# Gate and up products in two fp16 terms instead of two fp32r terms

## The chip, the cores and the metric

The kernel runs on one core of a Trainium2 chip. The metric is the device time of one execution in microseconds (us), lower is better, as the median of several runs.

## The reference

A block of memory-augmented attention and a gated feed-forward layer read the same x and are mixed by a gate. All inputs are fp32.

```python
x: [1, 2048, 576]; 32 heads of 18; 4 segments of 512 rows; F = 4608
g = sigmoid((x * gate_w).sum(-1))
# a: in each segment softmax(q k^T) v, mixed by sigmoid(beta) with what a running
#    memory M = sum phi(k)^T v gives for phi(q); then @ wo
# b:
b = (silu(x @ w_gate) * (x @ w_up)) @ w_down
out = g * a + (1 - g) * b
```

The change is in b: the gate and up products x @ w_gate and x @ w_up, [2048, 576] x [576, 4608] each.

## The kernel before

**Two terms.** TensorE multiplies fp32r, a rounded form of fp32 that takes 4 bytes. To keep the precision of fp32, an operand is split: `split` (L114) copies it to a high term in fp32r on ScalarE (L115) and subtracts that from the source on VectorE for a low term (L116). A product is then three matmuls: high x high, high x low, low x high. The 64 rows of the contraction over 576 that are left after four tiles of 128 are packed: high, low and a repetition stand in one tile of 96 or 128 rows, so that one matmul does them.

**Stage one, segments 0 to 3** (0 to 222 us of the profile, `for s in range(NSEG)`, L564). In each segment nine chains of 14 products (`qk`, products at L138) make q and k, with the update of the memory (`upd_gen`) between chains, and eight value steps (`v_step`, L342) make v, from segment 1 on with reads of the memory (`mem_step`). Work of other engines that is to lie beside a chain is put into the list `mid`, which `qk` calls. In segments 0 to 2 the remainder rows of x for the feed-forward layer are split (`rest_load`, `rest_sum`, `rest_split`, L509 to L526; those of the second half are stored in `xrd`), and the remainder rows of the first 8 tiles of weights (`b_step`). In segment 3, x of the first half is loaded, summed and split (`first_load`, `first_sum`, `first_split`).

**Stage two, the loop over f** (222 to about 1700 us, L1043). Rows of x are taken in two halves of 1024, F in 36 tiles of 128. The gate and up products of one half and one f are made by a Strassen scheme with seven products: `seven` (L1030) does one of them with six matmuls of 128x512 (L1035) and one for the remainder rows (L1038), all fp32r. Sums and differences of weight blocks are made by GpSimd, split (`w_make`, L239: ScalarE L251, VectorE L254) and stored in `wc` for the second half, which fetches them (`w_fetch`). Remainder weights go the same way through `rc` (`r_block`, `r_fetch`). The seven results are combined by copies and sums in three PSUM banks (L1093 to L1119); the gate goes through Silu, is multiplied with up, and the product is split again (`hh`, `hl`). The down products (`down_part`, L874) follow for three f at a time.

Between two `seven` stands one `tick`, which calls `beat`: it first issues what `defer(k, ...)` has put off to this beat, then down products, then a step of attention (`att_gen`; scores at L706 and L753 in bf16, values at L782 and L784 in fp16 and bf16). All engines run their instructions in the order written; there is no scheduler that moves them.

x for the second half is loaded, summed and split around the change of halves (`x_second`), into the same tiles `xo..` (`x_slot(SLOT[j], z)`) that held the first half's operands; ten beats of down products and attention (`BREAK`) cover that.

**The end** (about 1700 to 1782 us). Attention's result is multiplied with wo, mixed with the feed-forward result (`f_load` fetches the first half's) and stored.

Of the kernel before, what the change touches and what calls it, by code (L numbers as in the profile page):

```python
# [15 lines left out]
F16 = mybir.dt.float16  # L16
AF = mybir.ActivationFunctionType
# [3 lines left out]
P = 128  # L21
# [31 lines left out]
SLOT = (0, 3, 2, 1, 4, 6, 5)  # L53
RPOS = (0, 1, 4, 2, 5, 6, 3)
BLOCKS = {3: (4, 5), 6: (6, 7), 9: (8, 9), 12: (10, 11), 15: (12,), 18: (13,), 21: (14,), 24: (15,), 27: (16,), 30: (17,)}
KR = 6 * DH

# [6 lines left out]
def gated_mix(ctx, tc, xT, xrest, wf, wfr, wfh, wd, wv, wo, beta, cmask, ident, bmask, out):  # L64
# [30 lines left out]
    consts.tile([P, 16], F32, name="gap")  # L95
    xo = pool(ctx, "xo", 1)
# [17 lines left out]
    def split(hi, lo, src):  # L114
        nc.scalar.activation(hi, src, AF.Copy)  # L115
        nc.vector.tensor_sub(lo, src, f32(hi))  # L116

# [27 lines left out]
    def xr_tile(j, dtype=F32R):  # L145
        return xo.tile([P, L], dtype, name=f"xr{j}")
# [68 lines left out]
    def op_tile():  # L215
        return wop.tile([P, 2, 2, P], F32R, name="wo_")

    def r_block(h, o):
        i, c = divmod(h, 2)
        a, t = (rp.tile([P, 7, 64], d, name=z, bufs=1) for d, z in ((F32, "rr"), (F32R, "rt")))  # L220
# [7 lines left out]
        def keep(k):  # L228
            d = rc[i, 32 * k:32 * k + 32].rearrange("r f (j n) -> (r f) j n", n=P)
            nc.sync.dma_start(d[:, :, 64 * c:64 * c + 64], f32(t))  # L230

        return [(o, lambda: nc.sync.dma_start(a[:, 0:4], wfh[h - 4])), (o + 2, sums),
                (o + 3, lambda: nc.scalar.activation(t, a, AF.Copy)), (o + 3, lambda: keep(0)), (o + 3, lambda: keep(1)),
                (o + 4, lambda: nc.vector.tensor_sub(t, a, f32(t))), (o + 5, lambda: keep(2))]

    def r_fetch(f):
        nc.sync.dma_start(f32(rhs[f % 2][:96]).rearrange("p j n -> p (j n)"), rc[f // 4, :, f % 4])

    def w_make(f):  # L239
# [9 lines left out]
        def high(j):  # L249
            ops[j] = op_tile()  # L250
            nc.scalar.activation(ops[j][:, 0], src[j], AF.Copy)  # L251

        def low(j):
            nc.vector.tensor_sub(ops[j][:, 1], src[j], f32(ops[j][:, 0]))  # L254

        def keep(j):
            nc.sync.dma_start(wc[f, j], f32(ops[j]).rearrange("p a k n -> p (a k n)"))
# [12 lines left out]
    with ExitStack() as st:  # L270
# [178 lines left out]
        nc.vector.memset(vf[:, :, :, DH:E], 1.0)  # L449
        for i in range(2):  # L450
# [38 lines left out]
        def first_load(n):  # L489
            for q, (b, kt) in enumerate((((0, 0), (1, 0)), ((1, 2), (0, 1)), ((1, 1), (1, 3)), ((0, 2), (0, 3)))[n]):  # L490
                if n < 3:
                    r = qps[1].tile([P, NT * P], F32, name=f"{('qhi', 'qlo')[q]}{n}0")[:, :L]
# [10 lines left out]
        def first_split(j, z):  # L503
            XO[j][z] = x_slot(SLOT[j], z)
            split(XO[j][z][:, 0], XO[j][z][:, 1], rx[{1: (0, z), 4: (1, z), 2: (1, 2 + z), 6: (0, 2 + z)}[j]])
# [3 lines left out]
        def rest_load(h):  # L509
            for b in range(2):  # L510
                t = staging()[:, :2 * L].rearrange("p (a n) -> p a n", n=L)
                nc.sync.dma_start(t, xrest[HALF[h][b]])
                rr[b, 0], rr[b, 1] = t[:, 0], t[:, 1]
# [6 lines left out]
        def rest_split(h, j):  # L520
            raw = rr[((0, 0), (0, 0), (1, 1), (0, 1), (1, 0), (1, 1), (0, 1))[j]]
            XR[j] = xr_tile(j)
            nc.scalar.activation(XR[j], raw, AF.Copy)
            nc.vector.tensor_sub(XR[j][32:64], raw[32:64], f32(XR[j][32:64]))
            if h:
                late.append((xrd[j], f32(XR[j])))  # L526
# [5 lines left out]
        def b_load(i):  # L532
            rb[i] = xr_tile(6 * (i % 2), F32).rearrange("p (j n) -> p j n", n=P)
            nc.sync.dma_start(rb[i], wfr[i])

        def b_sums(i):
            a, b = rb[i], xr_tile(1, F32).rearrange("p (j n) -> p j n", n=P)
# [6 lines left out]
        def b_split(i, z):  # L544
            n = 4 - z
            src = (rb, rs)[z].pop(i)[:, :n].rearrange("p j n -> p (j n)")
            hi, lo = (xr_tile(k + z)[:, :P * n] for k in (2, 4))
# [693 lines left out]
```

## Time and profile before

| | |
|---|---|
| median of 3 runs | 1784.82 us (1784.69 to 1784.87) |
| span of the profiled execution | 1782.1 us, some 2.7 us under the median of the runs |
| TensorE (PE) busy | 1770.7 us, 99% of the span |
| VectorE (DVE), ScalarE (ACT), GpSimd (POOL) busy | 1281.8, 939.6, 831.9 us |
| matmuls / instructions in all | 12381 / 36452 |
| moved by DMA | 352 MB |

The page gives each engine's busy time, slices of the span, the chain of work that ended last (followed back from the last instruction), and groups of instructions by line of the kernel with count, busy time, mean duration and idle time before them. Matmuls are pipelined: one lasts longer than the distance to the next, so that what a product costs is read from start to start. PEld is the loading of weights into TensorE, which overlaps with products. L1035 is line 1035 of the kernel.

### The profile page before, as it was taken

To read this page: it belongs to the slowest core of one execution; us is meant where nothing else is said; L and a number is where in the kernel's file an instruction comes from. 1 tells how busy PE (TensorE), PEld (TensorE's weight loads), DVE (VectorE), ACT (ScalarE), POOL (GpSimd) and SP (SyncE) were. 2 spreads that over 40 slices of the span, in tenths; PEclk is the share of its full clock that TensorE was granted. 3 is DMA by queue.
4 is the path that set the end of the run, shared out by engine and by line. 5 is a ranking of instruction groups with operands and counts; after the bars stand their busy time and mean duration, and the time that the engine had idled before them with its cause. 6 is when DMAs were issued, how large, how long until landed. Compare 5 with 4: busy or idle time off the path is not lost.

```text
span 1782.1 us, 36452 instructions
## 1 busy us (share of the span) xinstructions
PE 1770.7 (99%) x12381; PEld 1521.5 (85%) x12381; DVE 1281.8 (72%) x3309; ACT 939.6 (53%) x1718; POOL 831.9 (47%) x1064
## 2 busy tenths in 40 slices
PE   9999999999999999999999999999999999999999
PEld 7899978888888888888887887887887887888899
DVE  6657666878877777777777777777777778775455
ACT  7766565455645564556456445445445445445411
POOL 4434731444554455445535555555555555454121
PEclk9999999999999999999999999999999999999999
DMA  8645497677657865776496447547546456545644
GB/s 298 212 176 184 153 344 225 189 249 264 217 176 238 265 201 174 243 249 215 137 339 207 153 136 215 150 130 215 155 138 210 141 151 195 160 126 188 204 141 140
DMA packets 249418, 352.02 MB, mean 198 GB/s; under 512 B 90320, under 2 KB 130640, under 8 KB 249232
## 3 DMA queue, kind: packets, MB, share of 16 engines
q1 hardware_dynamic: 249232, 349.69, 61.0%
q8 instruction: 98, 1.61, 0.4%
q14 instruction: 88, 0.72, 0.1%
HBM read 210.72 MB, written 138.87 MB: 196 GB/s over the span
## 4 chain that ended last, share of the span: by engine, by line
PE 94%; DVE 2%; DMA 2%; ACT 1%; issue 1%; SPq 0%; DVEq 0%; ACTq 0%
PE bank L1035 37%; PE bank L874 25%; PE bank L138 12%; PE bank L1038 6%; PE bank L753 4%; PE bank L706 4%; PE bank L782 2%; PE bank L784 1%; PE bank L423 1%; PE bank L377 1%; DMA rh<-rc 1%; DMA wo__23740<-wc 0%; PE bank L947 0%; PE bank L385 0%; DMA draw<-in_wd_dram 0%
## 5 line engine op out<-in xcount | busy, mean ns | idle before, releaser
L874 PE MATMUL bank<-dw,hh 128*128 128x320 f32 (+1 forms) x2304 | 485.8, 303 | 1.6 <-DVE ya L883 1.0
L845 POOL TENSOR_TENSOR p<-pe,p 128x512 f16<-128x512 f32 x320 | 381.1, 1191 | 176.3 <-DVE p L843 115.6
L874 PEld LDWEIGHTS bank<-dw,hh 128*128 128x128 f32 x2304 | 378.1, 189 | 19.2 <-DVE ya L883 2.4
L757 ACT ACTIVATE pe<-bank 128x512 f32<-128x512 f32 x320 | 190.4, 595 | 363.5 <-PE bank L753 333.4
L874 PE MATMUL bank<-dw,hl 128*128 128x320 f32 (+1 forms) x1152 | 340.4, 295 | 1.0 <-DVE hl L116 1.0
L765 POOL TENSOR_SCALAR_AFFINE_SELECT pe<-pe 128x256 f32<-128x256 f32 (+1 forms) x320 | 140.3, 438 | 274.1 <-ACT pe L757 270.7
L713 DVE CUSTOM_DVE_ANT_0 scr<-bank,cm 128x512 bf16<-128x512 f32 (+3 forms) x512 | 247.5, 483 | 20.3 <-PE bank L706 12.3
L883 DVE TENSOR_TENSOR ya<-bank,ya 128x320 f32<-128x320 f32 x352 | 157.1, 452 | 102.1 <-PE bank L874 100.2
L874 PEld LDWEIGHTS bank<-dw,hl 128*128 128x128 f32 x1152 | 217.6, 189 | 1.5 <-DVE hl L116 1.5
L1038 PE MATMUL bank<-xr,rh 128*128 128x512 f32 x504 | 196.3, 390 | 0.9 <-DMA rh<-rc 0.9
L753 PE MATMUL bank<-qst,kst 111*128 111x512 bf16 (+3 forms) x512 | 151.5, 305 | 0.0
L843 DVE CAST p<-pe 128x512 f16<-128x512 f32 x320 | 150.3, 470 | 0.0
L706 PE MATMUL bank<-kst,qst 108*128 108x512 bf16 (+3 forms) x512 | 126.1, 300 | 0.4 <-DVE mb L713 0.4
L247 POOL TENSOR_TENSOR ws<-raw 128x256 f32<-128x256 f32 x72 | 66.7, 926 | 110.2 <-DMA raw<-in_wf_dram 53.8
L973 DVE TENSOR_TENSOR hl<-row,hh 128x512 fp32r<-128x512 f32 x120 | 102.0, 850 | 22.1 <-ACT hh L972 21.7
L1038 PEld LDWEIGHTS bank<-xr,rh 128*128 128x128 f32 x504 | 94.6, 188 | 21.6 <-issue 1.3
L1103 ACT ACTIVATE row<-bank 128x512 f32<-128x512 f32 x72 | 43.1, 599 | 125.7 <-PE bank L1038 125.7
L1108 DVE TENSOR_TENSOR row<-bank,row 128x512 f32<-128x512 f32 x72 | 49.7, 691 | 79.9 <-ACT bank L1107 79.9
L1118 DVE TENSOR_TENSOR row<-bank,row 128x512 f32<-128x512 f32 x72 | 49.6, 689 | 60.4 <-PE bank L1038 58.7
L1107 ACT ACTIVATE bank<-bank 128x512 f32<-128x512 f32 x72 | 41.9, 582 | 96.6 <-PE bank L1038 96.6
L138 PE MATMUL bank<-xo,qhi 128*128 128x512 f32 x288 | 91.0, 396 | 0.4 <-DVE xo L116 0.4
L753 PEld LDWEIGHTS <-kst 111*128 111x128 bf16 x512 | 48.3, 97 | 43.3 <-issue 24.8
(1688 smaller groups left out, 3997.9 us busy)
## 6 DMA issues: line engine op xcount, KB each, us to landing
rh<-rc SPq DMA_DIRECT2D x72, 336.0 KB
dc<-dw SPq DMA_DIRECT2D x36, 576.0 KB
dw<-dc SPq DMA_DIRECT2D x36, 576.0 KB
raw<-in_wf_dram SPq DMA_DIRECT2D x72, 256.0 KB
stk<-q SPq DMA_DIRECT2D x32, 384.0 KB
draw<-in_wd_dram SPq DMA_DIRECT2D x36, 288.0 KB
rc<-rt SPq DMA_DIRECT2D x42, 224.0 KB
vd<-vps SPq DMA_DIRECT2D x8, 912.0 KB
```

Of the source, the lines that this page charges most:

```text
L138: nc.tensor.matmul(t, st[n], mv[n], start=(n == 0), stop=(n == 13))
L706: nc.tensor.matmul(t[:, c:c + w], qs[:KR, pr, P * i:P * i + P], ks[:KR, pr, 0:w], start=True, stop=True)
L713: nc.vector.tensor_tensor_reduce(scr[:, :w], t[:, c:c + w], cm[:, L - w:L], 1.0, -3.0e38, OP.add, OP.max, m[:, k:k + 1])
L753: nc.tensor.matmul(t[:, c:c + w], ks[:KR + 3, pr, P * j:P * j + P], qs[:KR + 3, pr, P * j:L], start=True, stop=True)
L757: nc.scalar.activation(pe, t, AF.Exp, scale=SCALE)
L765: nc.gpsimd.affine_select(d, d, pattern=pat, compare_op=OP.is_ge, fill=0.0, base=0, channel_multiplier=-1)
L843: nc.vector.tensor_copy(p1, pe)
L845: nc.gpsimd.tensor_sub(p2, pe, p1)
L874: nc.tensor.matmul(t, p, q[:, cs], start=(f == CH * c and n == 0), stop=(f == CH * c + CH - 1 and n == 2))
L883: nc.vector.tensor_add(ya[:, i, cs], t, ya[:, i, cs])
L1035: nc.tensor.matmul(t, w[:, p, z], x[z][:, q], start=first and n == 0, stop=False, skip_group_check=True)
L1038: nc.tensor.matmul(t, rem[:, RPOS[j]], XR[j], start=False, stop=True, skip_group_check=True)
```

## The change

- The operands of `seven`, weights and x, become fp16: a high term fp16(k * a) and a low term fp16(k * a - high). Before splitting they are scaled by a power of two k: `sx` for x, `sw[i]` for each group of four f. Count and shape of the matmuls are the same. The tiles, `wc` and `rc` take half the bytes.
- The powers are found on the chip. `square` sums squares along a row on ScalarE, `total` adds these sums on VectorE, `power` adds over the partitions with a one-column matmul against ones and makes a power of two from the exponent bits. For x this reads the tiles of segments 0 to 2. The weights of the first 8 f are loaded for it in segment 1 (`look`), those of the others in the first half's loop (`glance`: one group of four f ahead of its use, 2 or 3 loads and squares in each f from pos 0 to 20).
- The scale is taken out again: `iw` = 1 / (sw * sx) is the scale of the Silu, and of the split of w_down (`d_split`).
- Splits use `scalar_tensor_tensor` (source times k, minus the high term) in place of a subtraction.
- First half: j = 0, 3 and 5 used tiles of segments 2 and 3 as they stood; they now have splits of their own. The remainder rows of the first half are loaded and split in segment 3, those of the second half in the loop from pos FT - 6 on (`rest_second`); `xrd` is gone. The two steps j = 6 move from after the value steps into them.
- Remainder weights (`b_step`) move from segments 0 and 1 to segment 2.
- With half the bytes, the x operands of both halves fit side by side (`PLACE`, `x_home`), so those of the second half have homes of their own.

```diff
+TOP = 2.0 ** 76
+SX, SW, IW, ONE = 101, 102, 111, 120
+PLACE = ([[(2, z, 1) for z in range(2)], [(3, z, 0) for z in range(2)], ...
-    wc = dram.tile([FT, 7, P, 4 * P], F32, name="wc")
-    rc = dram.tile([FT // 4, 96, 4, 7 * P], F32, name="rc")
-    xrd = dram.tile([7, P, L], F32, name="xrd")
+    wc = dram.tile([FT, 7, P, 4 * P], F16, name="wc")
+    rc = dram.tile([FT // 4, 96, 4, 7 * P], F16, name="rc")
+    def split_16(hi, lo, src, k):
+        nc.scalar.activation(hi, src, AF.Copy, scale=k)
+        nc.vector.scalar_tensor_tensor(lo, src, k, hi, op0=OP.mult, op1=OP.subtract)
+    def square(src, c):
+        n = src.shape[1]
+        nc.scalar.activation(junk[:, :n], src, AF.Square, accum_out=sc[:, c:c + 1])
+    def total(out, a, b):
+        nc.vector.tensor_reduce(out, sc[:, a:b], axis=AX.X, op=OP.add)
+    def power(out, t):
+        nc.tensor.matmul(t, one.to_broadcast([P, P]), out, start=True, stop=True)
+        nc.vector.tensor_scalar_max(out, t, 1e-24)
+        bits = out.bitcast(I32)
+        nc.vector.tensor_scalar(bits, bits, 24, 127, op0=OP.logical_shift_right, op1=OP.bitwise_xor)
+        nc.vector.tensor_single_scalar(bits, bits, 23, OP.logical_shift_left)
+        nc.vector.tensor_scalar_mul(out, out, TOP)
+    def back(i):
+        nc.vector.tensor_mul(iw[i], sw[i], sx)
+        nc.vector.reciprocal(iw[i], iw[i])
+    def x_home(h, j, z):
+        a, b, c = PLACE[h][j][z]
+        if (a, b) not in homes:
+            homes[a, b] = xo.tile([P, 4, L], F16, name=f"xo{a}{b}")
+        return homes[a, b][:, 2 * c:2 * c + 2]
     def op_tile():
-        return wop.tile([P, 2, 2, P], F32R, name="wo_")
+        return wop.tile([P, 2, 2, P], F16, name="wo_")
         def high(j):
             ops[j] = op_tile()
-            nc.scalar.activation(ops[j][:, 0], src[j], AF.Copy)
+            nc.scalar.activation(ops[j][:, 0], src[j], AF.Copy, scale=sw[f // 4])
         def low(j):
-            nc.vector.tensor_sub(ops[j][:, 1], src[j], f32(ops[j][:, 0]))
+            nc.vector.scalar_tensor_tensor(ops[j][:, 1], src[j], sw[f // 4], ops[j][:, 0], op0=OP.mult, op1=OP.subtract)
         def first_split(j, z):
-            XO[j][z] = x_slot(SLOT[j], z)
-            split(XO[j][z][:, 0], XO[j][z][:, 1], rx[...])
+            XO[j][z] = x_home(0, j, z)
+            src = rx[((0, z), (0, z), (1, 2 + z), (0, 2 + z), (1, z), (1, 2 + z), (0, 2 + z))[j]]
+            split_16(XO[j][z][:, 0], XO[j][z][:, 1], src, sx)
-        FSUM = {4: [(1, 0), (4, 0)], 5: [(2, 0), (1, 1)], 7: [(4, 1), (2, 1)]}
-        FSPLIT = {6: [(1, 0), (4, 0)], 7: [(2, 0), (1, 1)], 8: [(4, 1), (2, 1)]}
+        FSUM = {5: [(1, 0), (4, 0)], 6: [(2, 0), (1, 1)], 8: [(4, 1), (2, 1)]}
+        FSPLIT = {4: [(0, 0)], 5: [(5, 0), (0, 1)], 6: [(1, 0), (4, 0)], 7: [(5, 1), (2, 0), (1, 1)], 8: [(3, 0), (3, 1)]}
...
+                if s == 3:
+                    if n == 1:
+                        mid.append(lambda: total(sx, 0, 20))
+                    if n == 2:
+                        mid.append(lambda: power(sx, lone_tile([P, 1])))
+                        rest_load()
+                        for i in range(2):
+                            mid.append(lambda i=i: back(i))
...
-                    for j, b, kt in ((0, 2, z), (3, 2, 2 + z), (5, 3, 2 + z)):
-                        XO[j][z] = xs_of[b][0][kt]
...
         def d_split(f, r):
-            split_by(1, d[:, 0], d[:, 1], r)
+            k = iw[f // 4]
+            defer(1, lambda: nc.scalar.activation(d[:, 0], r, AF.Copy, scale=k))
+            defer(2, lambda: nc.vector.scalar_tensor_tensor(d[:, 1], r, k, f32(d[:, 0]), op0=OP.mult, op1=OP.subtract))
         def f_load(n):
-            ff = x_slot(n // 2, n % 2, F32).rearrange("p a b -> p (a b)")[:, :D]
+            ff = x_slot(2 + n // 2 if n < 6 else 0, n % 2, F32).rearrange("p a b -> p (a b)")[:, :D]
+        def glance(i, k):
+            f, u = 4 * i + k // 2, k % 2
+            box = []
+            def load():
+                box.append(x_slot(6, k % 2, F32).rearrange("p a b -> p (a b)")[:, :NT * P])
+                nc.sync.dma_start(box[0].rearrange("p (k n) -> p k n", n=P), wf[f][:, u])
+            return [(0, load), (4, lambda: square(box[0], 20 + 9 * i + k))]
+            i = 2 + pos // 3
+            if half == 0 and i < FT // 4:
+                for n in range(3 if pos % 3 < 2 else 2):
+                    plan += [(o + 3 * n - n // 2, fn) for o, fn in glance(i, 3 * (pos % 3) + n)]
+            if half == 0 and pos % 3 == 0 and pos and i <= FT // 4:
+                plan += [(0, lambda i=i: total(sw[i - 1], 11 + 9 * i, 19 + 9 * i)),
+                         (1, lambda i=i: power(sw[i - 1], ts_tile([P, 1]))), (2, lambda i=i: back(i - 1))]
+            if pos == FT - 6:
+                plan += [(o, fn) for o, fn in rest_second(XR2)]
-            nc.scalar.activation(sg0, sg0, AF.Silu)
+            nc.scalar.activation(sg0, sg0, AF.Silu, scale=iw[f // 4])
-            nc.scalar.activation(sg1, y, AF.Silu)
+            nc.scalar.activation(sg1, y, AF.Silu, scale=iw[f // 4])
```

More of the change, by code (lines that the diff above doesn't have):

```diff
@@ L95, in gated_mix @@
     consts.tile([P, 16], F32, name="gap")
+    sc = consts.tile([P, 128], F32, name="sc")
+    junk = consts.tile([P, 640], F16, name="junk")
+    one, sx = sc[:, ONE:ONE + 1], sc[:, SX:SX + 1]
+    sw = [sc[:, SW + i:SW + i + 1] for i in range(FT // 4)]
+    iw = [sc[:, IW + i:IW + i + 1] for i in range(FT // 4)]
     xo = pool(ctx, "xo", 1)
@@ L518, in rest_sum, with rest_split @@
             nc.gpsimd.tensor_sub(o, p, q)
[L520 to L526, printed above, removed]
+        def rest_split(j):
+            XR[j] = xr_home(0, j)
+            rest_16(XR[j], rr[((0, 0), (0, 0), (1, 1), (0, 1), (1, 0), (1, 1), (0, 1))[j]])
         XR = [None] * 7
@@ L656, in gated_mix @@
             start.pop(0)[1]()
-        for z in range(2):
-            first_split(6, z)
     with ExitStack() as st:
```

152 lines of the change are left out of this document (106 added, 46 removed).

## The prediction

> **What bounds the kernel now.** I read the page first: its shares, its slices and the chain of work that ended last.
>
> ```profile
> PE 1770.7 (99%) x12381; PEld 1521.5 (85%) x12381; DVE 1281.8 (72%) x3309; ACT 939.6 (53%) x1718; POOL 831.9 (47%) x1064
> PEclk9999999999999999999999999999999999999999
> PE 94%; DVE 2%; DMA 2%; ACT 1%; issue 1%; SPq 0%; DVEq 0%; ACTq 0%
> PE bank L1035 37%; PE bank L874 25%; PE bank L138 12%; PE bank L1038 6%; PE bank L753 4%; PE bank L706 4%; PE bank L782 2%; PE bank L784 1%; PE bank L423 1%; PE bank L377 1%; DMA rh<-rc 1%; DMA wo__23740<-wc 0%; PE bank L947 0%; PE bank L385 0%; DMA draw<-in_wd_dram 0%
> ```
>
> TensorE is idle 11.4 us of 1782.1, at full granted clock, and 94% of the chain is its own. The lines that change (L1035 and L1038, `seven`) hold 43% of the chain. So a nanosecond saved on each of their products is a nanosecond of the end, as long as the other engines keep up; and no gain can come from waits beyond those 11.4 us. The question is what one such product costs, from start to start. For that I read TensorE in order of time.
>
> ```profile
> 901.01 1.54 PE L1035 MATMUL bank<-xo,wo__11855 128*128 128x512 f32 x6
> 902.39 0.39 PE L1038 MATMUL bank<-xr,rh 128*128 128x512 f32 x1
> 902.62 1.52 PE L1035 MATMUL bank<-xo,wo__11871 128*128 128x512 f32 x6
> 903.98 0.39 PE L1038 MATMUL bank<-xr,rh 128*128 128x512 f32 x1
> 904.20 0.30 PE L874 MATMUL bank<-dw,hh 128*128 128x320 f32 x1
> ...
> 1001.06 0.40 PE L874 MATMUL bank<-dw,hh 128*128 128x256 f32 x2
> 1001.30 0.28 PE L874 MATMUL bank<-dw,hl 128*128 128x256 f32 x1
> 1001.42 0.40 PE L874 MATMUL bank<-dw,hh 128*128 128x256 f32 x2
> ...
> 1001.90 0.38 PE L706 MATMUL bank<-kst,qst 108*128 108x512 bf16 x1
> 1002.12 0.27 PE L753 MATMUL bank<-qst,kst 111*128 111x256 bf16 x1
> ```
>
> Fourteen 4-byte products of 512 columns fill 901.01 to 904.20: 228 ns each, back to back. Three 4-byte products of 256 columns fill 1001.06 to 1001.42: 120 ns each. So 256 columns cost 108 ns, 512 cost 216, and a 4-byte product carries 12 ns that do not depend on its columns. A 2-byte product of 512 columns (L706) starts 0.22 us before the next one.
>
> ```profile
> L1038 PE MATMUL bank<-xr,rh 128*128 128x512 f32 x504 | 196.3, 390 | 0.9 <-DMA rh<-rc 0.9
> L753 PE MATMUL bank<-qst,kst 111*128 111x512 bf16 x128 | 50.0, 390 | 0.0
> L706 PE MATMUL bank<-kst,qst 108*128 108x512 bf16 x128 | 48.7, 381 | 0.4 <-DVE mb L713 0.4
> L1038 PEld LDWEIGHTS bank<-xr,rh 128*128 128x128 f32 x504 | 94.6, 188 | 21.6 <-issue 1.3
> L753 PEld LDWEIGHTS <-kst 111*128 111x128 bf16 x512 | 48.3, 97 | 43.3 <-issue 24.8
> ```
>
> These rows group products and weight loads by shape. At 512 columns the 4-byte product lasts 390 ns, the 2-byte one of L706 381 ns. The L753 one lasts 390, no less than the 4-byte one; at 512 columns it opens its attention step and so follows a 4-byte product, while L706 follows another 2-byte one. A 2-byte weight load lasts 97 ns against 188.
>
> **The change part by part.**
>
> *The products.* 2 halves x 36 x 7 x 7 = 3528 products of 512 columns become 2-byte; their number and columns stay. Saving per product: nothing if they behave like L753's (390 against 390), 12 ns if the whole fixed part goes, 9 ns by L706 (390 - 381, and 228 - 219). I take 9, since six of the seven products of a `seven` follow another 2-byte product, as L706's do: 3528 x 9 = 31.8 us, between 0 and 42.3.
>
> The Trainium skill ("TensorE: Matmul & The Clock Gate", Back-to-back issue gap) gives N / 2.4 + 2.5 ns from start to start, 215.8 ns at 512 columns, with no type in it. The trace's 4-byte 228 ns disagrees with that; if the formula holds for 2-byte products alone, the saving by it is an estimate of 12 ns and 43 us.
>
> *Where types meet.* In the order written out, the stream changes between 4-byte and 2-byte operands 533 times instead of 667, since attention's 2-byte products now stand next to the gate and up products. I price an entry at the 9 ns that L753 shows above L706; 67 pairs of changes fewer are 0.6 us saved.
>
> *Scales on the chip.* Ten one-column products (`power`) stand in TensorE's order. The nearest rows are its four 128-column transposes in 0.44 us (L385), 0.11 us each: 1.1 us. Each waits for VectorE's sum, issued one chain or one tick before it, so I add nothing for the wait; queued behind it are the next products, and if VectorE came 0.5 us late each time it would be 5 us.
>
> ```profile
> 118.52 0.44 PE bank L385 x4
> ```
>
> *Stage one's last segment.* The remainder splits of the first half move into it, and j = 0, 3, 5, which used to borrow the fp32r tiles of x, need splits of their own. The windows are its last chains and its value steps, then two stretches of the loop over f and two disturbed places.
>
> ```profile
> 181.00:202.00 21.00, 21.00 (x115) 18.27 (x114) 9.47 (x19) 10.51 (x19) 14.92 (x16) 1.00 0.37 119
> 202.00:222.00 20.00, 20.00 (x150) 19.66 (x150) 16.31 (x47) 11.37 (x32) 16.77 (x20) 1.00 0.53 186
> 222.00:501.00 279.00, 275.78 (x1672) 236.45 (x1671) 210.71 (x500) 159.76 (x318) 112.16 (x161) 1.00 0.75 251
> 501.00:898.00 397.00, 397.00 (x2695) 344.50 (x2694) 302.66 (x767) 223.14 (x433) 193.47 (x251) 1.00 0.64 211
> 898.00:928.00 30.00, 29.41 (x185) 26.48 (x183) 22.90 (x39) 12.44 (x22) 11.71 (x8) 1.00 1.02 350
> 1660.00:1700.00 40.00, 37.95 (x207) 32.54 (x207) 22.23 (x37) 15.89 (x29) 7.72 (x8) 1.00 0.75 239
> ...
> L116 DVE TENSOR_TENSOR xo<-xo,xo 128x512 fp32r<-128x512 f32 x16 | 12.2, 770 | 2.8 <-ACT xo L115 2.8
> L116 DVE TENSOR_TENSOR xo<-qhi,xo 128x512 fp32r<-128x512 f32 x2 | 2.5, 1238 | 0.0
> L115 ACT ACTIVATE xo<-xo 128x512 fp32r<-128x512 f32 x16 | 9.8, 615 | 0.4 <-DMA xo<-in_xT_dram 0.3
> L518 POOL TENSOR_TENSOR xo<-xo,xo 128x512 f32<-128x512 f32 x6 | 8.5, 1420 | 7.8 <-DVE xr L524 7.8
> ```
>
> The columns after the length are TensorE, weight loads, VectorE, ScalarE, GpSimd. In the chains 11 splits (7 + 6 - 2 that go later) are added, in the value steps 4. ScalarE: 10.51 + 11 x 0.615 = 17.3 of 21 us, room. GpSimd: 14.92 + 4 x 1.42 = 20.6 of 21, just full. VectorE at 0.77 us a split: 9.47 + 8.5 + 16.31 + 3.1 = 37.4 of 41, room; at the 1.24 us that splits of x took in this very stretch (the row with qhi): 9.47 + 13.6 + 16.31 + 5.0 = 44.4 of 41, 3.4 us too much. TensorE waits for VectorE there through its banks, so the bounds are 0 and 5 us; I take 3, by the second row.
>
> The Trainium skill ("GPSIMD Engine Reference", Specifications) says GpSimd's SBUF ports contend with VectorE instructions of two SBUF inputs; 1.24 against 0.77 us agrees, and the new splits still have two such inputs, so by it too the larger figure is the one for this stretch.
>
> *Squares in the loop.* 56 squares of 640 columns (`glance`) are added in the first 21 f; the nearest row is a 640-column copy of 0.73 us: 41 us of ScalarE over some 395 us (21 of 36 f in the 676 us from 222 to 898).
>
> ```profile
> L115 ACT ACTIVATE qhi<-xo 128x640 fp32r<-128x640 f32 x9 | 6.6, 731 | 2.2 <-DMA xo<-in_wf_dram 2.2
>   ACT bank L1093: 2.2, 4
> ...
> L329 DVE TENSOR_TENSOR qr<-bank,q 128x512 f32<-128x512 f32 x36 | 24.8, 688 | 52.3 <-ACT ph L327 38.2 <-ACT q L322 11.6 <-POOL q L333 2.3
> L335 DVE SCALAR_TENSOR_TENSOR ph<-bank,ph 128x512 f32<-128x512 f32 x28 | 19.2, 687 | 0.2
> ```
>
> ScalarE runs there at 57% (159.76 of 279) and goes to 68%. What covers a square is the next `seven` (1.6 us) with what stands between: `a` is copied out at L1093 and is written again only after the next `seven`. Products waited for that copy 4 times, 2.2 us in all. I add 2 us for squares in front of it, 0 to 6. The second half's seven remainder splits, moved from stage one to f = 30 on, find ScalarE at 56% (223.14 of 397): nothing.
>
> Another 38 squares lie in segments 0 to 2.
>
> ```profile
> 88.00:145.00 57.00, 57.00 (x352) 51.87 (x351) 35.69 (x89) 38.02 (x78) 23.62 (x26) 1.00 0.46 160
> ```
>
> At 0.615 us they are 23 us, the 14 remainder copies that leave are 8.6; 15 us more over three segments of some 57 us take ScalarE's 67% to 75%, and three banks of a chain lie between it and TensorE: nothing, 0 to 1 us.
>
> *Splits by scale.* `scalar_tensor_tensor` takes the place of a subtraction: 687 against 688 ns. VectorE, 75% busy at most in the loop, gains nothing and loses nothing.
>
> *Transfers.* Stored operands are halved (wc, rc) and xrd goes; 23 MB of weights are read once more for the squares (72 loads of 256 or 320 KB). With x's second operands in their own homes, their splits no longer wait for the first half's last products. The two disturbed windows hold 0.6 and 2.05 us of idle; I take 1.5 us off, between 0 and 2.7.
>
> *Sum.* - 31.8 - 0.6 + 1.1 + 3 + 2 - 1.5 = - 27.8 us. The profiled span is 1782.1 us, the median 1784.82 (2.7 more, the same before and after): 1757 us.
>
> **The rivals.**
>
> *The whole fixed part goes.* A product at 216 ns: - 42.3 in place of - 31.8, 1746.5 us. For it speaks that the weight load, 188 ns to 97, is all that differs beside the stream; against it that L706 shows 9.
>
> *Type makes no difference to a stream.* All products stay at 228 ns, as L753's 390 would have it: + 1.1 + 3 + 2 - 1.5 = 4.6 us slower, 1789.4. Against it: every 512-column L753 stands behind a 4-byte product. The skill's formula, read for all types alike, would give this as well; the 228 ns speak against that reading.
>
> *Helpers run out.* TensorE waits in stage one and at the copies of L1093 for 10 to 20 us more: 1767 to 1777. For it: GpSimd's 20.6 of 21.
>
> *ScalarE in front of the copies, the other side.* If each of the 56 squares stands fully ahead of a copy that TensorE waits for, they cost 41 us in place of 2: 1757 + 39 = 1796. It turns the sign when more than 40 of the 56 do ((27.8 + 2) / 0.73). Against it: 68% load, and `seven` lasts longer than two ScalarE operations.
>
> **How the numbers follow.** Forecast 50%, whole fixed part 24%, helpers 14%, no difference by type 6%, squares 6%. A difference of 0.2% (3.6 us) is about what a measurement of this kernel can tell from none. The forecast's own range is 1747 to 1766; the first three cases are faster, but 3 points of the helpers' go to an outcome near zero, as does 1 of the last two cases; so faster 0.85, same 0.04, slower 0.11. The range that keeps eight in ten reaches from 1743 (the whole fixed part and all waits at their best, 1784.8 - 42.3 - 0.6 + 1.1 - 2.7 = 1740, cut by its small chance) to 1777 (the helpers' worst).
>
> **What would show it.** In the profile after: products of `seven` fourteen in about 3.07 us; their mean near 381 and weight loads near 97; TensorE's idle time near 15 us; the window after stage one's chains longer by some 3 us; idle time at L1093 under 6 us. Wrong would be: fourteen still in 3.19 us (type makes no difference), idle time of TensorE at 25 us or more (helpers), or ScalarE named as releaser of the products for tens of us (squares).

## The result and the profile after

| | before | after |
|---|---|---|
| median of the runs | 1784.84 us (1784.69 to 1785.90, 4 runs) | 1838.38 us (1833.56 to 1843.47, 4 runs) |
| ratio, 95% interval | | 1.030 (1.028 to 1.032) |
| profiled execution, span | 1782.1 us | 1841.8 us (that run took 1843.47) |
| mean granted TensorE clock | 1.000 | 0.983 |
| TensorE idle in the span | 11.4 us | 80.1 us |
| moved by DMA | 352 MB | 286 MB |

The change makes the kernel 3.0% slower; forecast were 1757 us, within 1743 to 1777. None of the rivals reaches the measured time either; the dearest of them was priced at 1796 us. The profiled execution is 5 us above the median of its kernel; the balance below is made against its span, 59.7 us more than before. (A correction to the section on the change: `sx` reads tiles of all four segments, those of segment 3 in its first two chains.)

The shares, the granted clock by slices and the chain of the page after:

```profile
PE 1761.7 (96%) x12401; PEld 1240.5 (67%) x12401; DVE 1332.9 (72%) x3383; ACT 1046.0 (57%) x1912; POOL 839.0 (46%) x1065
PEclk9999999899999999999999999999999999999999
PE 75%; ACT 8%; DVE 6%; issue 4%; DMA 4%; SPq 1%; POOL 1%; ACTq 0%; DVEq 0%; POOLq 0%
```

Over the whole span no helper engine has come near its limit: ScalarE stands at 57%, VectorE at 72% (the end of stage one is another matter, see below). What has changed is that 25% of the chain now lies outside TensorE, against 6% before. The list of waits of TensorE says for whom (total us, times, longest):

```profile
PE bank L140 <- DVE sc L137: 25.4, 8, 3.9
PE bank L1151 <- ACT bank L1219: 17.2, 11, 3.2
PE bank L171 <- DVE r L409: 6.5, 1, 6.5
```

L140 and L137 are the matmul of `power` and the sum of `total` before it; L1151 and L1154 are the products of `seven` (L1035, L1038 before), L1219 the copy of `a` (L1093 before); L171 are products of chains and value steps. All but 0.4 us of these waits lie in the first 700 us. Two windows, the loop where it searches for scales and most of the second half (TensorE is the first column behind the length, the clock stands behind the five engines):

```profile
247.00:700.00 453.00, 407.27 (x2494) 259.25 (x2493) 318.09 (x770) 284.55 (x553) 171.63 (x237) 0.95 0.62 192
...
1010.00:1660.00 650.00, 647.66 (x5236) 433.38 (x5235) 510.35 (x1487) 345.08 (x551) 356.33 (x456) 1.00 0.42 121
```

From 247 to 700 TensorE is idle for 45.7 of 453 us and the clock is 0.95; in the second half it is idle for 2.3 of 650 us, at full clock.

I then took the trace of each kernel apart by f: from the last remainder product of one f to that of the next (36 f in each half; "start" is the first product of `seven`). Differences to before, in us, for the kernel after and the ten experiments:

| | start (before: 220.0) | f 0 to 21 | f 22 to 28 | f 29 to 32 | f 33 to 35 | second half | end |
|---|---|---|---|---|---|---|---|
| after | +20.6 | +56.7 | -2.5 | +8.1 | -0.2 | -23.4 | +0.3 |
| e1_none | +20.8 | -7.3 | -2.6 | +7.7 | -0.2 | -23.3 | +0.1 |
| e2_late_power | +20.6 | +49.8 | -0.4 | +9.0 | -0.2 | -23.3 | -0.6 |
| e3_fill | +19.7 | +37.3 | -2.6 | +8.3 | -0.2 | -23.6 | +0.1 |
| e4_early_loads | +21.1 | +46.6 | -2.6 | +7.5 | -0.2 | -23.2 | -0.9 |
| e5_move | +20.5 | +9.6 | -2.0 | +8.0 | -0.2 | -22.9 | +0.1 |
| e6_order | +9.1 | +57.8 | -2.6 | +7.8 | -0.2 | -22.7 | -1.0 |
| e7_all | +9.2 | +6.2 | -1.9 | +8.0 | -0.2 | -23.2 | -0.9 |
| e8_const | +11.1 | -4.1 | -2.5 | +8.0 | 0.0 | -22.1 | +0.1 |
| e9_best | +10.2 | -6.1 | +1.6 | +1.8 | -0.2 | -24.4 | -0.9 |
| e10_best2 | +10.9 | -6.6 | -2.6 | +1.9 | +0.9 | -24.1 | -0.9 |

The first row adds up to 59.6 of the 59.7 us. Of its 56.7 us, 37.4 lie in f = 0, 3, ..., 21 (from f = 3 on these are the "long" f, with down products, and each of the seven holds a power), 17.1 in f = 2, 5, ..., 20 and 2.1 in the others.

**The products did what they were to do.** The second half, in order of time:

```profile
1105.29 1.46 PE L1151 MATMUL bank<-xo,wo__13928 128*128 128x512 f16 x6
1106.58 0.38 PE L1154 MATMUL bank<-xr,rh 128*128 128x512 f16 x1
1106.80 1.46 PE L1151 MATMUL bank<-xo,wo__13930 128*128 128x512 f16 x6
```

Seven products take 1.51 us, 216 ns each against 228. The Trainium skill's N / 2.4 + 2.5 ns ("TensorE: Matmul & The Clock Gate", Back-to-back issue gap), which it gives for a product by itself, is 215.8; the trace agrees for 2-byte operands.

**Why the power waits.** The chain of waits around one power, in order of time (start, us, what):

```profile
483.44 0.70 ACT junk L134 x2
...
484.16 0.07 ACT L1144
484.23 1.23 issue
485.46 0.03 ACT bg L1144
...
485.57 0.58 ACT bank L1219
486.15 0.42 ACT wo__5453 L307
486.57 0.53 ACT hh L125
...
487.12 0.04 DVE hl L126
...
487.73 0.17 DVE sc L137
...
487.94 0.38 PE bank L140 x2
```

The sum at L137 takes 0.17 us and its squares have long been there. But it stands in VectorE's queue behind `hl` (L126), which waits for `hh` (L125); `hh` stands in ScalarE's queue behind a square, the table load for exp (484.16 to 485.46) and two copies. TensorE meets the power right behind the `seven` and waits for all of that:

```profile
487.94 0.38 PE L140 MATMUL bank<-sc 128*128 128x1 f32 x2 [3.32 <-DVE sc L137]
```

The chain from table load to `hl` was there before as well (59 + 58 such loads in both kernels, 1.28 us each): as I read the order, down products and the next `seven` covered it. The power is the first thing on TensorE that needs VectorE's queue to be empty at that moment.

**Why the copy waits.** In f = 5, ScalarE, then TensorE:

```profile
335.92 0.74 ACT L134 ACTIVATE junk<-xo 128x640 f16<-128x640 f32 x1 [1.36 <-DMA xo<-in_wf_dram]
...
336.65 0.76 ACT L946 ACTIVATE dw<-draw,sc 128x576 fp32r<-128x576 f32 x1
337.32 0.57 ACT L1219 ACTIVATE bank<-bank 128x512 f32<-128x512 f32 x1
```

```profile
337.94 1.85 PE L1151 MATMUL bank<-xo,wo__3633 128*128 128x512 f16 x6 [2.86 <-ACT bank L1219]
```

The square has to wait for its load, and the split of w_down and the copy stand behind it.

**A second cost of each wait.** After a wait TensorE runs at half clock for a while. Consecutive windows of 3.41 us:

```profile
413.96:417.37 3.41, 1.77 (x9) 0.59 (x6) 2.63 (x5) 3.16 (x7) 0.75 (x1) 1.00 0.87 328
417.37:420.79 3.42, 1.40 (x8) 0.81 (x9) 1.77 (x7) 2.57 (x6) 1.51 (x4) 1.00 0.84 252
420.79:424.20 3.41, 3.41 (x13) 2.74 (x12) 1.99 (x6) 0.00 (x0) 0.00 (x0) 0.50 0.68 229
424.20:427.61 3.41, 3.41 (x24) 2.59 (x23) 3.12 (x13) 0.91 (x2) 0.96 (x2) 1.00 0.02 3
```

TensorE does 13 products in the third window and 24 in the fourth. The trace has 14 such stretches from 117 to 690 us, ten of 3.413 and four of 6.827 us, 61.4 us in all. At half the rate they cost up to 30.7 us, an estimate. TensorE is idle 68.7 us more than before (80.1 - 11.4); both together, less the 36 to 42 us that the products save (below), make 57 to 63 us, and 59.7 were measured.

**Stage one.** VectorE in segment 3's value steps:

```profile
214.56 4.03 DVE L197 SCALAR_TENSOR_TENSOR xr<-xr,sc,xr 32x512 f16<-32x512 f32 x1
218.63 3.08 DVE L130 SCALAR_TENSOR_TENSOR xo<-xo,sc,xo 128x512 f16<-128x512 f32 x3
...
222.35 0.74 DVE L197 SCALAR_TENSOR_TENSOR xr<-xo,sc,xr 32x512 f16<-32x512 f32 x1
223.12 2.30 DVE L130 SCALAR_TENSOR_TENSOR xo<-ph,sc,xo 128x512 f16<-128x512 f32 x2
225.34 0.44 DVE L409 TENSOR_TENSOR r<-bank,vps 128x288 f32<-128x288 f32 x1
```

and TensorE behind it:

```profile
225.84 1.57 PE L171 MATMUL bank<-vw,xo 128*128 128x288 f32 x5 [6.54 <-DVE r L409]
```

Seven splits stand on VectorE ahead of the sum at L409 that frees TensorE's bank. Here VectorE is full: it is busy for 28.3 of the 30 us from 196 to 226 us, and GpSimd for 16.8 of the first 17. Around the powers of stage one TensorE waits for 0.7, 1.9 and 1.8 us (twice in segment 2, once in segment 3), and half clock follows at both places, 3.4 us each, as it follows the long wait, 6.8 us.

### The profile page after: what moved, and what is told of

It is laid out like the page before. It is cut to its first block, busy times and chain, and to the rows that moved or that the text cites. A ratio compares the mean times of both kernels' runs of the same rounds, so it can differ in the third digit from the quotient of the medians.

```text
span 1841.8 us, 36811 instructions
## 1 busy us (share of the span) xinstructions
PE 1761.7 (96%) x12401; PEld 1240.5 (67%) x12401; DVE 1332.9 (72%) x3383; ACT 1046.0 (57%) x1912; POOL 839.0 (46%) x1065
## 4 chain that ended last, share of the span: by engine, by line
PE 75%; ACT 8%; DVE 6%; issue 4%; DMA 4%; SPq 1%; POOL 1%; ACTq 0%; DVEq 0%; POOLq 0%
PE bank L1151 25%; PE bank L965 23%; PE bank L171 10%; PE bank L1154 4%; PE bank L842 4%; PE bank L795 4%; DMA xo<-in_wf_dram 2%; PE bank L871 2%; ACT junk L134 1%; PE bank L873 1%; PE bank L433 1%; ACT bank L1219 1%; ACT dw L946 1%; ACT row L1238 1%; DVE scr L802 1%
## 5 line engine op out<-in xcount | busy, mean ns | idle before, releaser
L965 PE MATMUL bank<-dw,hh 128*128 128x320 f32 (+1 forms) x2304 | 514.5, 316 | 6.5 <-DVE ya L974 5.4
L965 PEld LDWEIGHTS bank<-dw,hh 128*128 128x128 f32 x2304 | 384.1, 192 | 33.8 <-DVE ya L974 8.2
L854 POOL TENSOR_SCALAR_AFFINE_SELECT pe<-pe 128x256 f32<-128x256 f32 (+1 forms) x320 | 144.5, 452 | 286.4 <-ACT pe L846 281.0
L1154 PE MATMUL bank<-xr,rh 128*128 128x512 f16 x504 | 194.0, 385 | 0.3 <-POOL mq L785 0.3
L1064 DVE TENSOR_TENSOR hl<-row,hh 128x512 fp32r<-128x512 f32 x120 | 108.5, 904 | 21.3 <-ACT hh L1063 21.3
L1234 DVE TENSOR_TENSOR row<-bank,row 128x512 f32<-128x512 f32 x72 | 49.8, 691 | 66.8 <-ACT bank L1233 66.6
L171 PE MATMUL bank<-xo,qhi 128*128 128x512 f32 x288 | 92.8, 403 | 0.6 <-DVE xo L126 0.4
L1154 PEld LDWEIGHTS <-rh 128*128 128x128 f16 x504 | 49.9, 99 | 61.9 <-issue 3.0
L389 POOL TENSOR_TENSOR q<-qr,q 128x512 bf16<-128x512 f32 x36 | 44.0, 1221 | 91.6 <-ACT q L388 83.8
```

Source lines behind the costliest of these rows:

```text
L171: nc.tensor.matmul(t, st[n], mv[n], start=(n == 0), stop=(n == 13))
L854: nc.gpsimd.affine_select(d, d, pattern=pat, compare_op=OP.is_ge, fill=0.0, base=0, channel_multiplier=-1)
L965: nc.tensor.matmul(t, p, q[:, cs], start=(f == CH * c and n == 0), stop=(f == CH * c + CH - 1 and n == 2))
L1154: nc.tensor.matmul(t, rem[:, RPOS[j]], XR[j], start=False, stop=True, skip_group_check=True)
```

## The experiments

The theory after the comparison: the products saved about what they could, and the loss has three sources, each with waits and half clock behind them: the search for scales in the loop, the added splits and powers in stage one, the remainder splits moved into f = 30 to 32. Rivals: the fp16 operations themselves are dearer for the helpers (then the loss stays without the search), or the squares load ScalarE (then it stays when only the powers move).

**e1_none: no search in the loop.**

```diff
+    sw, iw = sw[:2] + 7 * sw[1:2], iw[:2] + 7 * iw[1:2]
...
-                    plan += [(o + 3 * n - n // 2, fn) for o, fn in glance(i, 3 * (pos % 3) + n)]
...
-                plan += [(0, lambda i=i: total(...)), (1, lambda i=i: power(...)), (2, lambda i=i: back(i - 1))]
```

> Groups 2 to 8 of the weights take group 1's scale: the loop's 56 loads and squares, its seven sums and powers go; stage one and f = 30 on stay. Theory (waits): f = 1 to 21 lost 57.4 us against before and would gain some 0.35 us each undisturbed, so 65 us go: about 1773 us, clock 0.99. Rival (the fp16 splits and their load on VectorE and ScalarE are what holds TensorE): most of the loss stays, 1820 us or more.

Measured 1778.91 us, ratio 0.998 (0.997 to 0.998). f 0 to 21 go from +56.7 to -7.3 us: the search in the loop costs 64 us of the profiled execution, and the splits, loads and products that stay cost little in these f, which gain 0.33 us each where those of the second half gain 0.65. The time is 6 us above the expectation; what stays are stage one (+20.8) and f 29 to 32 (+7.7). So the first rival falls: the fp16 operations that are left do not hold up these f.

**e2_late_power: five beats between sum and power.** The remainder weights, which need the scale, move by four beats as well.

```diff
-                         (1, lambda i=i: power(...)), (2, lambda i=i: back(i - 1))]
+                         (5, lambda i=i: power(...)), (6, lambda i=i: back(i - 1))]
-                    plan += r_block(h, 4 * n)
+                    plan += r_block(h, 4 * n + 4)
```

> Only the place of the loop's seven powers: five beats after the sum instead of one (remainder blocks four beats later). Theory (waits): the seven waits of 3.5 to 4.3 us go, 25 us, and with them the half clock that follows each, 31 us of half clock, worth about 15: 1798 us. Rival (ScalarE and VectorE have too much to do, wherever the product stands): the wait moves to another product, 1830 us or more.

Measured 1840.66 us, ratio 1.032 (1.031 to 1.034): a miss. The wait of the powers for the sum, 25.4 us, is down to 0.7, but others have come up:

```profile
PE bank L1151 <- ACT bank L1219: 21.6, 14, 2.8
PE bank L965 <- DVE ya L974: 9.0, 10, 2.5
```

The long f fall from +37.4 to +20.3 us, the others rise from 19.2 to 29.6. The last steps of the remainder weights now fall into f = 4, 5, 7, 8 and so on; as I read it, sevens without down products between them cover less. What was won at one place was lost at the next. Since powers and remainder weights moved in one edit, the run does not tell what the place of the powers alone is worth.

**e3_fill: no half clock.** Fourteen products on an idle tile ahead of each power of the loop, to keep TensorE busy while it waits; they add nothing to the result.

```diff
-    def power(out, t):
+    def power(out, t, fill=0):
+        for _ in range(fill):
+            nc.tensor.matmul(t[:, :L], junk[:, :P], junk[:, :L], start=True, stop=True)
```

> Fourteen junk products of 512 columns (3.0 us) stand ahead of each of the loop's seven powers, so that TensorE works through the wait instead of idling. Theory (waits, and a clock that halves after some 3 us of idling): the wait costs as much as before, but the half clock after it goes, about 15 us: 1823 us, with no half clock in the loop after a power. Rival (the clock has no part): 1838 us, or more by what the products last beyond the wait.

Measured 1822.84 us, ratio 1.022 (1.021 to 1.024), as expected. The filling took the place of the wait almost one for one:

```profile
PE bank L143 <- DVE sc L137: 3.8, 8, 0.7
...
L141 PE MATMUL bank<-junk 128*128 128x512 f16 x98 | 22.3, 380 | 0.1
```

98 products at 216 ns are 21.2 us in place of 21.6 us of waiting (25.4 - 3.8), so what the kernel gained, 14 us by the ratios and 15.5 by the medians, is the clock's. Five stretches of half clock are left of 14.

**e4_early_loads: squares with loads one f ahead**, into six tiles in place of two.

```diff
-            return [(0, load), (4, lambda: square(box[0], 20 + 9 * i + k))]
...
+                plan += glances(pos, 4, glance) + glances(pos + 1, 0, glance_load)
```

> Each load of a square in the loop is issued eight beats earlier, into six tiles in place of two; squares and powers stay in their places. Theory (squares wait for their load on ScalarE and hold the copy of a behind them): the stalls of f = 2, 5, 8, ..., 20 go, 17 us and three half-clock stretches of 3.4 us: 1815 to 1822 us. Rival (ScalarE has too much to do): within 5 us of 1838.

Measured 1830.80 us, ratio 1.026 (1.024 to 1.028). Right in kind, smaller in size: f = 2, 5, ..., 20 fall from +17.1 to +7.1 us, f = 5, 11 and 14 from 4.27, 4.35 and 3.17 to 1.11, 1.11 and 0.41, but the wait at the copy keeps 11.7 of its 17.2 us. The load was part of it. The rest I put on the square itself in an f too short to cover it; e5, which takes the squares out of these f, bears that out.

**e5_move: the whole search of a group in one long f**, the power in the next f.

```diff
+            if half == 0 and pos % 3 == 0 and 2 <= i < FT // 4:
+                plan += glance(i)
+                plan += [(10, lambda i=i: total(sw[i], 20 + 9 * i, 28 + 9 * i)),
+                         (14, lambda i=i: power(sw[i], ts_tile([P, 1]))), (16, lambda i=i: back(i))]
```

> The loop still finds all scales, in other places: the eight loads and squares of a group lie in one f with down products (32 us) instead of three f, its sum two beats into the next f, its power four beats after that; remainder blocks three f later. Theory (waits that come from the place): f = 1 to 21 run as without the squares, within 0.5 us each: 1775 to 1785 us. Rival (the amount of work on ScalarE and VectorE): waits move to the long f and it stays above 1805.

Measured 1797.46 us, ratio 1.007 (1.006 to 1.009). The same 56 squares and seven powers cost 17 us (9.6 + 7.3) in place of 64, and f = 2, 5, ..., 20 lose nothing in sum. So it is less ScalarE's load or the operations that cost than the places where they stand, and the second rival falls as well. That it is 17 and not nothing lies mostly in the long f (+11.4 us, where e1 has -1.8): TensorE now waits there for attention's copies behind the eight squares:

```profile
PE bank L795 <- ACT pe L846: 10.2, 12, 1.5
```

**e6_order: stage one and the remainder rows.** The first two weight scales are found in segment 1's value steps and right behind them, that of x in segment 2's, segment 3's loads, sums and splits start two chains earlier, and the second half's remainder splits stand three beats apart from f = 28 on.

```diff
-        RSTEP = {4: (0, 3, -1), 5: (5, -4, 1), 6: (-2, 4), 7: (2, -6), 8: (6,)}
+        RSTEP = {2: (0, 3), 3: (-1, 5), 4: (-4, 1), 5: (-2, 4), 6: (2, -6), 7: (6,)}
...
+                    if n == 4:
+                        total(sw[0], 20, 29)
+                    if n == 6:
+                        power(sw[0], y_tile([P, 1]))
...
-            return todo + [(5 + n, lambda j=j: step(j)) ...
+            return todo + [(5 + 3 * n, lambda j=j: step(j)) ...
```

> Outside the loop's squares, order alone: the first two weight scales found in segment 1's value steps; x's squares of segment 3 and its scale in segment 2's value steps; loads, sums and splits of segment 3 begin two chains earlier; the second half's remainder steps three beats apart from f = 28 on. Theory (waits): of stage one's 20.6 us some 15 come back (first product of the loop at 226 us or before) and f = 30 to 32 lose under 1 us instead of 8.4: about 1838 - 15 - 8 = 1815. Rival (splits of fp32 into fp16 beside GpSimd take VectorE too long wherever they stand): the first product stays at 235 us or later.

Measured 1831.08 us, ratio 1.027 (1.025 to 1.028). 16 us above the expectation: the start gives back 11.5 us; f 29 to 32 nothing, their waits only moved (f = 29 now +3.3 and f = 30 +2.6, where f = 30 had +4.4).

**e7_all: e5 and e6 together.**

> e5 and e6 together. Theory (waits): both gains add, about 1838 - 55 - 23 = 1760, and clock near 1.0. Rival (amount of work): above 1784.

Measured 1782.89 us, ratio 0.999 (0.998 to 1.000). The parts add up (start +9.2, f 0 to 21 +6.2), and so does what e5 and e6 had each left, 23 us above the expectation: f 29 to 32 still lose 8.0, and the start 9.2. Of the versions that still find every scale this is the fastest, and it is level with the kernel before.

**e8_const: nothing found at all**, scales as constants, splits as the change has them.

```diff
+        nc.gpsimd.memset(sc[:, SX:SX + 1], 128.0)
+        nc.gpsimd.memset(sc[:, SW:SW + 2], 256.0)
...
```

> Nothing is found on the chip: all scales are constants (2^7 for x, 2^8 for the weights), so squares, sums, powers and the loads for them are gone, in stage one too; the splits stay where the change put them, and group 1's scale serves all f, as in the run without a search in the loop (1778.9, loop starting at 240.8 against 220.0 before). Theory A, stage one loses its 20 us in two parts, waits for the powers (5 us in segment 2, 2 us and half clock in segment 3) and VectorE's slow splits beside GpSimd in segment 3 (some 11 us): the loop starts near 231, and the time is about 1769. Rival B, the squares and sums on ScalarE and VectorE are all of it: start near 221, time about 1759. Rival C, the splits alone are all of it: start near 239, time about 1777.

Measured 1771.02 us, ratio 0.992 (0.991 to 0.994); the loop starts at 231.1, as theory A has it. So of stage one's 20.6 us 9.5 are the search's, and 11.1 belong to the splits and what else was moved there. VectorE's slow split and the long wait of the value steps stand as they did:

```profile
205.38 4.02 DVE L198 SCALAR_TENSOR_TENSOR xr<-xr,sc,xr 32x512 f16<-32x512 f32 x1
```

```profile
216.64 2.77 PE L172 MATMUL bank<-vw,xo 128*128 128x288 f32 x10 [6.52 <-DVE r L410]
```

**e9_best: no search in the loop, e6's stage one, remainder rows of the second half in long f.** Group 1's scale serves all f, as in e1; a kernel for other weights would have to find one scale for all of them ahead.

```diff
-            return todo + [(5 + n, lambda j=j: step(j)) ...
+            return todo + [((5, 6, 7, 24, 25, 26, 27, 28, 29, 30, 48)[n], lambda j=j: step(j)) ...
-            if pos == FT - 6:
+            if pos == FT - 9:
```

> No search in the loop (group 1's scale for all f), the powers of stage one found earlier and with a chain between sum and power, segment 3's splits two chains earlier, and the second half's remainder rows loaded in f 27 and split only in the long f 27, 30 and 33. If the parts add up: 1778.9 for no search in the loop, less 12 to 14 for the start (229 or a little less against 240.8), less 5 to 7 of the 8 us that f 30 to 32 lost: about 1760 (1757 to 1765), faster than before by 1.2 to 1.5%. Rival: the remainder splits only move their waits, as they did when spread over more beats: 1766.

Measured 1765.74 us, ratio 0.989 (0.987 to 0.990), 0.7 us above the expected range and at the rival's 1766. f 29 to 32 fall from +7.7 (e1) to +1.8, but f = 27 now loses 4.0, so that most of these waits have only moved. ScalarE and VectorE there:

```profile
750.56 1.28 ACT L1152 ACT_TABLE_LOAD   x1
751.85 0.20 ACT L1152 ACTIVATE bg<-idt 128x1 f32<-128x1 f32 x1
751.96 0.49 ACT L308 ACTIVATE wo__9828<-ws,sc 128x256 f16<-128x256 f32 x1
752.36 0.70 ACT L197 ACTIVATE xr<-xo,sc 128x512 f16<-128x512 f32 x1
```

```profile
753.10 0.74 DVE L198 SCALAR_TENSOR_TENSOR xr<-xo,sc,xr 32x512 f16<-32x512 f32 x1 [3.96 <-ACT xr L197]
```

It is the power's pattern again: VectorE takes up an operation whose source stands on ScalarE behind the table loads, and everything behind it on VectorE waits too. The kernel after has the same wait of 3.96 us in f = 30, at 884.80.

**e10_best2: ScalarE's half in one beat, VectorE's in the next.**

```diff
-                    rest_16(rest[j], rr[...])
+                    nc.scalar.activation(rest[j], raw, AF.Copy, scale=sx)
+                    defer(1, lambda: nc.vector.scalar_tensor_tensor(rest[j][32:64], raw[32:64], sx[32:64], ...))
...
+            return todo + [((24, 25, 26, 26, 27, 28, 47, 48, 49, 50, 51)[n], lambda j=j: step(j)) ...
```

> As the last combined version, but the second half's remainder rows are copied by ScalarE in one beat and subtracted by VectorE one beat later, all in the long f 30 and 33, with the loads in f 27. In the last version VectorE waited 3.96 us for such a copy, which stood on ScalarE behind two table loads (747.96 to 752.36), and TensorE 2.7 and 1.4 us with it. Theory: a VectorE instruction issued in the same beat as its ScalarE source waits whenever the table loads of Silu and exp fall in that beat; with a beat between them f 27 to 35 lose under 1 us, where the last version lost 4.0 in f 27 and 2.8 in f 30: 1765.7 - 6 = about 1760. Rival: any work added there costs what it costs, wherever its halves stand: 1765 to 1767 again.

Measured 1763.74 us, ratio 0.988 (0.987 to 0.990). f = 27 is free again (-0.2 where it had +4.0), but that doesn't show the theory: e9 has two of the seven splits in f 27, four in f 30 and one in f 33, e10 has none, four and three. In f = 30, with four splits in both, VectorE hardly waits for ScalarE ahead of them (at most 0.34 us in e9, 0.03 in e10), and TensorE still loses +2.8 in e9 and +3.0 in e10:

```profile
796.01 0.74 DVE L1138 SCALAR_TENSOR_TENSOR xr<-xo,sc,xr 32x512 f16<-32x512 f32 x1
```

```profile
797.33 0.56 PE L973 MATMUL bank<-dw,hh 128*128 128x320 f32 x2 [1.52 <-DVE ya L982]
```

Here the split itself stands ahead of the sum (`ya`, L982) that TensorE waits for; what is left is not that wait for ScalarE. f = 33 has +0.9. Half of the expected 6 us came in the trace, and 2 of them in the median, which the two intervals can't tell from nothing; the rival stands. e10 and e9 are the fastest versions, 1.2 and 1.1% under before. e8 (0.992) and e1 (0.998) are under it too; all four leave out the search in the loop. Of the 36 us that the products save, some 11 are still spent in stage one.

## Why the prediction was wrong, step by step

**The products** (31.8 us, 9 ns each, bounds 0 to 42.3): right in kind, mis-sized low. Start to start it is 228 to 216 ns, the rival "the whole fixed part goes". In what an f costs where nothing else disturbs it, 9.9 us over 29 f of the first half in e1 and 23.3 over the second half's 36, that is 0.34 and 0.65 us per f, over all 72 some 36 us (12 ns for each of the 3528 would be 42.3). L706 against L1038 by mean duration understated it; the distance from start to start was the measure. Why the halves differ was not tried.

**Where types meet, -0.6 us.** The trace has the 533 changes in place of 667 that were counted; no run shows what one of them costs.

**Ten powers at 1.1 us, "so I add nothing for the wait".** This is the step that failed first. The wait for the sum was 25.4 us: 3.3 to 3.9 us in each of seven f, and 0.7 in segment 2. "VectorE's sum, issued one tick before it" is true, but what stands in VectorE's queue ahead of the sum was not followed: `hl`, and through it ScalarE's queue with a table load. My bound of 5 us was 0.5 us a time, taken from no row; the delay could have been read from the trace of before as the time at which VectorE gets through its queue in that beat.

**The clock** was not a term of the sum at all. e3 prices it at some 15 us for the powers' waits alone. The Trainium skill ("TensorE: Matmul & The Clock Gate", Why this matters for your kernels) warns of idle gaps over about 3 us; the trace agrees that waits cost clock, and shows it for shorter ones (below). In the profile of before no wait was long enough, so nothing there spoke of it; the prediction should have asked of each new wait whether it could.

**Squares in the loop, 2 us (0 to 6).** Failed too: 17.2 us at the copy, eight times the value taken, of which 2.1 stay without the squares (e1). The load on ScalarE was not the point: it was busy for 63% of f 0 to 20 (278 of 439 us), under the forecast's 68%. The rival "ScalarE in front of the copies" named the mechanism and had its price, 41 us, by the number of squares; it decided where the f is short or the square's load late. I let an average over 395 us stand for it, and did not follow the square's own DMA, four beats ahead.

**Stage one, +3 us (0 to 5).** 20.6. The row of 1.24 us was the right one to take, and still low. It is the mean of a split of 0.68 us with no GpSimd instruction beside it (194.57 in the trace of before) and one of 1.79 us beside GpSimd nearly throughout (199.09). In the kernel after, the first two rows below are splits of stage one, the third those of the second half:

```profile
L130 DVE SCALAR_TENSOR_TENSOR xo<-xo,sc,xo 128x512 f16<-128x512 f32 x10 | 12.9, 1325 | 0.2
L197 DVE SCALAR_TENSOR_TENSOR xr<-xr,sc,xr 32x512 f16<-32x512 f32 x3 | 6.4, 2138 | 0.1
L130 DVE SCALAR_TENSOR_TENSOR xo<-raw,sc,xo 128x512 f16<-128x512 f32 x7 | 5.4, 776 | 4.8 <-ACT xo L129 4.8
```

The sum spread VectorE's work over chains and value steps together, 44.4 of 41 us, and took 3 us for what was too much; the work had to be done where it stood, and half clock came on top. The search, put at nothing in segments 0 to 2, took 9.5 of the 20.6 us (e8); five of the 38 squares, and the power of x's scale, lie in segment 3.

**The second half's remainder splits: nothing.** 8.1 us in f 29 to 32. ScalarE is busy for 60% of f 30 to 32 (859 to 927 us), near the 56% of the forecast. With all of them in the long f 30 and 33 and a beat between their halves (e10), f 29 to 35 lose 2.8 us in place of 7.9, so that more than half of the loss was the order, not the amount of work.

**Transfers, -1.5 us.** Not seen in sum, though 66 MB less are moved. Of the two disturbed places the end of the second half has 1.1 us of idle (1737 to 1755 us) where it had 2.05, but the change of halves has 2.6 us (955 to 1012) where it had 0.6. Why the change of halves got longer was not tried.

**Splits by scale, nothing.** At 512 columns each costs some 0.07 us more. Like for like, the splits of x out of `raw` took 706 ns on VectorE before and 776 after (above):

```profile
L116 DVE TENSOR_TENSOR xo<-raw,xo 128x512 fp32r<-128x512 f32 x7 | 4.9, 706 | 4.8 <-ACT xo L115 4.8
```

The rows that the prediction compared, 687 and 688 ns, read a PSUM bank, which the splits do not. On ScalarE a copy with a scale took 712 ns where it took 615, which the prediction did not price. (The copies for w_down, whose type stays, took 766 ns with a scale and 677 without, so it is the scale.)

```profile
L129 ACT ACTIVATE xo<-xo,sc 128x512 f16<-128x512 f32 x10 | 6.8, 712 | 1.0 <-POOL xo L560 1.0
```

Of the three signs of "wrong" one came true, TensorE's idle time of 80 us where 25 was the mark, and one nearly: ScalarE is the named releaser of the products of `seven` for 19 us (17.2 at the copy and 2.1 at L1238), where the mark was tens. The rival "helpers run out" had the right sort of loss at 10 to 20 us, and at the end of stage one VectorE was indeed full. In the loop the helpers' queues lost it, at some 20 places, without any of them being full over the stretch.

## What to carry to other kernels

An instruction of TensorE that waits for a tiny result of another engine is priced by what stands in that engine's queue ahead of it, and in the queues behind that, not by the result; follow the queues back at the very place, above all past table loads, before writing zero. A new wait of two microseconds in a stream without gaps can be paid twice, as wait and as half clock. Side work with a long chain across engines belongs where the stream has cover: the same search cost 64 us spread over f 0 to 21 and 17 us with its squares in the long f (e5). That a beat between one engine's half and the next one's helps is not shown (e10).

## What was not expected of the hardware

- **The half clock comes on a fixed grid and for less than a long gap.** In each trace with such stretches every one begins a whole multiple of 3.413 us after the first. Cutting the traces of after and the ten experiments into these windows, between 20 and 1740 us: with TensorE idle for less than 1.76 us of a window at full clock the next one was never at half clock, with more than 2.0 us it always was, between these both occurred. In the rows above, 1.64 us idle (413.96) leaves the clock at 1.00, 2.02 us (417.37) halves it. The Trainium skill ("TensorE: Matmul & The Clock Gate", Part 1) describes a free-running window of 3413 ns and a drop after an idle one; the length agrees, but a window idle for little over half its time was enough here. So a wait costs clock or not by where it falls, which may be why the kernel after varies by 10 us (that link was only argued).
- **A VectorE instruction on 32 partitions took 4.03 us** (L197 at 214.56) and 0.74 at 222.35. GpSimd beside them:

```profile
214.40 1.28 POOL L580 TENSOR_TENSOR xo<-xo,xr 128x512 f32<-128x512 f32 x1
...
216.76 1.29 POOL L560 TENSOR_TENSOR xo<-xo 128x512 f32<-128x512 f32 x1
...
223.06 1.15 POOL L389 TENSOR_TENSOR q<-qr,q 128x512 bf16<-128x512 f32 x1 [1.89 <-ACT q L388]
```

The slow one lies beside three GpSimd operations back to back and ends 0.5 us after the last of them, the quick one in GpSimd's pause. Five splits of 128x512 between 196 and 212 us, beside GpSimd throughout, took 1.66 to 1.77 us each; one at 218.63, with none beside it, 0.75, but so did one at 226.91 beside GpSimd. No run took GpSimd's work away, so the cause is not shown.
